# A packing moved to ScalarE and two groups of products moved in TensorE's order, in an attention and FFN kernel

## The chip, the cores and the metric

The kernel runs on one core of one Trainium2 chip. The metric is device time in microseconds (us), lower is better. Before the change the median of the first three runs was 401.98 us (401.9 to 402.39).

The engines have short names in the profile: PE is TensorE (matrix products), PEld its weight loads, DVE is VectorE, ACT is ScalarE, POOL is GpSimd, SP is SyncE. DMA engines move data between HBM and the core; in this kernel SP and POOL issue all of those transfers but the last. "Banks" are the tiles in PSUM into which TensorE writes its products.

## The reference, cut to what matters

```python
k_proj = einsum('ks,bhsd->bhkd', E, k)              # 8 batches, 8 heads, 1024 rows of 64
v_proj = einsum('ks,bhsd->bhkd', F, v)
attn = softmax(q @ k_proj.T / 8)                    # 1024 x 64 a head
x = (attn @ v_proj) as (8192, 512)
out = max(x @ w1, x @ w2, x @ w3) @ w_out           # 512 -> 768 -> 512
```

## The kernel before

The FFN (feed-forward network, the last line above) is most of the work: for each half batch ("chunk", 512 rows) there are six "up" steps of 12 products (2.6 us each) and four "down" steps of 6 (1.3 us each). The attention of the next batch is hung into these steps. TensorE runs its instructions in the order in which the code emits them, so a product that has to wait holds up all that follow: below, the up products behind v of batch 3 do not read v, and yet they start at 129.80, after its wait of 0.71 us.

In the first batch, chunk 1 of q is packed (two heads side by side), transposed on TensorE and copied out. All of this stands between the products with the third up weight:

```python
def pack_q(b, gs, lo, nsi):
    def f():
        ...
        for g in gs:
            copy("v", q_pk[b][:, g, lo:lo + nsi]..., qkv[b][0][:, 2 * g:2 * g + 2, lo:lo + nsi], (), 0.25)
    return f

def qp(b, gs, lo, nsi):             # 8 transposes into a pair of PSUM banks, then one copy to qT on VectorE
    ...
    (2, "a", 0): [pack_q(0, (0, 1), *c1)],     # after the first two products of up step 0 ... 5
    (2, "a", 1): [pack_q(0, (2, 3), *c1)],
    (2, "a", 4): [qp(0, (0, 1), *c1)],
    (2, "a", 5): [qp(0, (2, 3), *c1)],
    (2, 1): [sc(0, 0, *c1)],                   # scores of head pair 0, after up step 1, and so on
    (2, 3): [sc(0, 1, *c1)],
    (2, 4): [za(0, 0, *c1, then=True), sc(0, 2, *c1)],
```

Later batches hang on loads that GpSimd issues, on output stores and on transposes by DMA that SyncE issues:

```python
# plan for batch 1, hung into batch 0 (chunk, step)
(0, 7): [qd(1, 2), za(0, 2, *c1)],   # qd: pack q on VectorE, transpose it by DMA into qT
(0, 8): [za(0, 3, *c1)],
(1, 0): [kproj(1)],                  # needs k of batch 1 in SBUF
(1, 2): [vproj(1), ld(2)],           # needs v of batch 1; ld(2) then loads batch 2 into the same tiles
(1, (3, "mid")): [sc(1, 0, now=True), sc(1, 1)],   # needs qT of batch 1
# plan for batch 3, hung into batch 2
(0, 1): [kproj(3), vproj(3), ld(4)],
(0, 2): [kt(3)],
(0, 3): [sc(3, 0, now=True), sc(3, 1)],
# in down(): after every second down step, 0.5 MB go out
elif tt % 2:
    nc.sync.dma_start(out=ov[:, si - 1:si + 1, :], in_=o_sb)
```

The softmax here doesn't subtract the row's maximum and nothing guards it: scores larger than these inputs give would overflow.

Of the kernel before, what the change touches and what calls it, by code (L numbers as in the profile page):

```python
# [15 lines left out]
def kernel(  # L16
# [70 lines left out]
    def pe(dt, wait=0.0):  # L87
        clock["pe"] = max(clock["pe"], wait) + dt
        return clock["pe"]
# [41 lines left out]
    qkv, qTs, kpTs, vps, pTs, zis, xTs = {}, {}, {}, {}, {}, {}, {}  # L131
# [73 lines left out]
    def scores(b, g, lo, nsi):  # L205
        t, ns = two()
        n = nsi // 2
        for c in range(2):
            for hp in range(2):
                rows = slice(hp * HALF, (hp + 1) * HALF)  # L210
                at = g * SI + lo + c * n
                nc.tensor.matmul(  # L212
                    out=t[c * HALF:(c + 1) * HALF, hp, 0:n * P],
                    lhsT=kpTs[b][rows, g, :],
                    rhs=qTs[b][rows, at:at + n, :],
                    start=True, stop=True,
                )
        return t[:, :, 0:n * P], ns, pe(n * MM / 4 + 0.1)
# [103 lines left out]
    def sc(b, g, lo=0, nsi=SI, now=False):  # L322
        def f():
            t = scores(b, g, lo, nsi)
            if now:
                exps(b, g, lo, nsi, t)
            else:
                later.append(lambda: exps(b, g, lo, nsi, t))
        return f
# [34 lines left out]
    q_pk = {}  # L364

    def pack_q(b, gs, lo, nsi):


        def f():
            if b not in q_pk:  # L370
                q_pk[b] = att.tile([P, NPAIR, SI, 2, D], BF16, name="q_p", bufs=1)
            for g in gs:
                copy(
                    "v", q_pk[b][:, g, lo:lo + nsi].rearrange("p si h d -> p h si d"),
                    qkv[b][0][:, 2 * g:2 * g + 2, lo:lo + nsi], (), 0.25,
                )
        return f

    def qp(b, gs, lo, nsi):
        def f():  # L380
            t, ns = two()
            t = t.bitcast(BF16)[:, 0]
            n = nsi * P
            for i, g in enumerate(gs):
                for si in range(nsi):
                    nc.tensor.transpose(
                        out=t[:, i * n + si * P:i * n + (si + 1) * P],
                        in_=q_pk[b][:, g, lo + si].rearrange("p h d -> p (h d)"),
                        identity=ident,
                    )  # L390
                pe(0.06 * nsi)
            o = qTs[b].rearrange("a (g si) p -> a g si p", si=SI)
            copy(
                "v", o[:, gs[0]:gs[-1] + 1, lo:lo + nsi, :],
                t[:, 0:len(gs) * n].rearrange("a (g si p) -> a g si p", si=nsi, p=P),
                ns, 0.1 + len(gs) * nsi * 0.08,
            )
        return f
# [20 lines left out]
    def kproj(b):  # L419
        def f():  # L420
            t, ns = bank()
            proj(b, 1, t, (LO, HI), 4 * D)
            kps[b] = att.tile([P, 2, 2 * D], BF16, name="kp")
            copy("v", kps[b].rearrange("a g x -> a (g x)"), t[:, 0:4 * D], ns, 0.43)
        return f

    def kt(b):
        def f():
            t, ns = two()
            t = t.bitcast(BF16)[:, 0]  # L430
            for gg in range(2):
                nc.tensor.transpose(
                    out=t[:, gg * P:(gg + 1) * P], in_=kps[b][:, gg, :], identity=ident
                )
            pe(0.2)

            kpTs[b] = att.tile([P, NPAIR, KP], BF16, name="kpT")
            copy(
                "v", kpTs[b].rearrange("a (y x) k -> a x y k", x=2),
                t[:, 0:2 * P].rearrange("a (x y k) -> a x y k", x=2, y=2), ns, 0.3,  # L440
            )
        return f

    def vproj(b):
        def f():
            t, ns = bank()
            proj(b, 2, t, (LO, HI), 4 * D)

            vps[b] = att.tile([P, H, D], BF16, name="vp")
            for hh, hs in enumerate((LO, HI)):  # L450
                i = t[hh * HALF:(hh + 1) * HALF, 0:4 * D].rearrange("a (h d) -> a h d", d=D)
                for to in range(2):
                    copy("sv"[hh], vps[b][to * HALF:(to + 1) * HALF, hs, :], i, ns, 0.4)
        return f
# [250 lines left out]
    def ld(b, which=(0, 1, 2)):  # L705
        return lambda: load(b, which)

    def plan(b):
        n = b + 1
        if b == 0:  # L710
            c1 = (SPC, SPC)
            return {
                (0, 6): [za(0, 1, *c1), sc(0, 3, *c1)],
                (0, 7): [qd(1, 2), za(0, 2, *c1)],
                (0, 8): [za(0, 3, *c1)],
                (1, 0): [kproj(1)],
                (1, 1): [kt(1)],
                (1, 2): [vproj(1), ld(2)],
                (1, (3, "mid")): [sc(1, 0, now=True), sc(1, 1)],
                (1, 4): [za(1, 0), sc(1, 2, now=True)],  # L720
                (1, 5): [za(1, 1), sc(1, 3)],
                (1, 7): [za(1, 2)],
                (1, 8): [za(1, 3)],
            }
        if b == 1:
            return {
                (0, 0): [qd(2)],
                (0, 3): [kproj(2), vproj(2), ld(3, (0,))],
                (0, 4): [kt(2)],
                (0, 5): [sc(2, 0, now=True), sc(2, 1, now=True), sc(2, 2)],  # L730
                (0, 6): [sc(2, 3)],
                (0, 8): [zc(2, nc.gpsimd), ld(3, (1, 2))],
                (1, 1): [qd(3)],
                (1, 3): [vx(2, 0), vx(2, 1)],
                (1, 6): [vx(2, 2), vx(2, 3)],
            }
        if b == 2:
            return {
                (0, 1): [kproj(3), vproj(3), ld(4)],
                (0, 2): [kt(3)],  # L740
                (0, 3): [sc(3, 0, now=True), sc(3, 1)],
                (0, 5): [sc(3, 2, now=True), sc(3, 3)],
                (0, 7): [zc(3)],
                (0, 8): [qd(4)],
                (1, 3): [kproj(4), vproj(4), ld(5), vx(3, 0), vx(3, 1)],
                (1, 4): [kt(4)],
                (1, 7): [vx(3, 2), vx(3, 3), sc(4, 0)],
            }
        if n == B:
            return {}  # L750
        out = {
            (0, 1): [sc(n, 1, now=True), sc(n, 2, now=True), sc(n, 3)],
            (0, 3): [zc(n)],
            (1, 2): [vx(n, 0), vx(n, 1)],
            (1, 6): [vx(n, 2), vx(n, 3)],
        }
        if n + 1 < B:
            out[0, 4] = [qd(n + 1)]
            out[1, 2] = [kproj(n + 1), vproj(n + 1)] + out[1, 2]
            out[1, 3] = [kt(n + 1)]  # L760
            out[1, 6] += [sc(n + 1, 0)]
        if n + 2 < B:
            out[1, 3] += [ld(n + 2)]
        return out

    for b in range(B):
        p = plan(b)

        def behind(ch, step):
            for f in p.get((ch, step), []):  # L770
                f()

        for ch in range(NCHUNK):
            if (b, ch) == (0, 0):
                c1 = (SPC, SPC)
                up_first({
                    (0, 0, 1): [lambda: x(1)],
                    (0, 0, 3): [lambda: z(2), lambda: z(3)],
                    (0, 1, 3): [lambda: v_pair(2), lambda: x(2)],
                    (0, 1, 5): [lambda: v_pair(3), ld(1)],  # L780
                    (0, 2, 1): [lambda: x(3)],
                    (2, "a", 0): [pack_q(0, (0, 1), *c1)],
                    (2, "a", 1): [pack_q(0, (2, 3), *c1)],
                    (2, "a", 4): [qp(0, (0, 1), *c1)],
                    (2, "a", 5): [qp(0, (2, 3), *c1)],
                    (2, 1): [sc(0, 0, *c1)],
                    (2, 3): [sc(0, 1, *c1)],
                    (2, 4): [za(0, 0, *c1, then=True), sc(0, 2, *c1)],
                })
                run_later()  # L790
                behind(0, NJT - 1)
            else:
                for step in range(NJT):
                    up(b, ch, step, lambda: behind(ch, (step, "mid")))
                    behind(ch, step)
            for tt in range(SPC):
                down(b, ch, tt, "v" if b == 0 else "s")
                behind(ch, NJT + tt)
# [30 lines left out]
```

## Time and profile before

| what | before |
|---|---|
| time, first three runs | 401.98 us median |
| time of the profiled execution | 402.96 us (span 401.0) |
| TensorE busy | 392.7 us, 98% |
| DMA engines, first 8 of 40 slices | 90% busy or more |

What TensorE's products waited for, before (total us, times, longest):

```profile
PE banks L346 <- DMA v_t<-in_v_dram: 0.7, 1, 0.7
...
PE banks L212 <- ACT zl L292: 0.5, 1, 0.5
PE banks L490 <- DMA k_t<-in_k_dram: 0.5, 1, 0.5
PE banks L386 <- DVE qT L102: 0.3, 1, 0.3
```

The timeline of TensorE, before, from 34 to 59 us (start, length, engine, line, operation, count; in brackets the idle time before it and what ended that):

```profile
34.66 0.61 PE L386 MATMUL banks<-ident,q_p 128*128 128x128 bf16 x8 [0.35 <-DVE qT L102]
...
39.08 0.30 PE L212 MATMUL banks<-qT,kpT 64*64 64x256 bf16 x4 [0.52 <-ACT zl L292]
...
39.76 1.46 PE L687 MATMUL banks<-wout_sb,hT 128*128 128x512 bf16 x6
...
49.33 1.06 PE L346 MATMUL banks<-k_t,efT 128*64 128x256 bf16 x16
...
55.72 1.06 PE L346 MATMUL banks<-v_t,efT 128*64 128x256 bf16 x16
...
58.55 0.63 PE L212 MATMUL banks<-qT,kpT 64*64 64x512 bf16 x8
```

The second transposes wait for the qT copy, the third scores wait for the Ln (the logarithm of the softmax sums, zl in the profile), the down products start at 39.76. Then k, v and the first scores of batch 1 come at 49.33, 55.72 and 58.55 with no wait. The k and v products of batch 3, in the same view:

```profile
127.03 1.06 PE L346 MATMUL banks<-k_t,efT 128*64 128x256 bf16 x16
128.80 1.06 PE L346 MATMUL banks<-v_t,efT 128*64 128x256 bf16 x16 [0.71 <-DMA v_t<-in_v_dram]
```

The two groups start 1.77 us apart, with a wait for the v load between them. VectorE does the four packings here, as its timeline shows:

```profile
32.82 0.89 DVE L102 COPY q_p<-q_t 128x512 bf16<-128x512 bf16 x4
```

### The profile page before, as it was taken

How to read it: one execution, taken by the hardware profiler on the slowest of the kernel's cores; microseconds unless marked ns; L12 is line 12 of the kernel's file. 1: busy time of each engine (PE TensorE's matmuls, PEld its weight loads, DVE VectorE, ACT ScalarE, POOL GpSimd, SP SyncE). 2: the span in 40 equal slices, each digit the busy share in tenths (PEclk: the TensorE clock that was granted, in tenths of full speed). 3: DMA queues.
4: the chain of work that ended last, by engine and by line, in shares of the span. 5: the costliest groups of instructions: out<-in, count | busy, mean ns of one | idle time of the engine just before them, and what ended most of it. 6: DMA issues, size and time to landing. Idle time of an engine off the chain costs nothing.

```text
span 401.0 us, 5752 instructions
## 1 busy us (share of the span) xinstructions
PE 392.7 (98%) x2286; PEld 176.6 (44%) x2286; DVE 204.1 (51%) x323; ACT 149.0 (37%) x238; POOL 34.4 (9%) x49
## 2 busy tenths in 40 slices
PE   8999999999999999999999999999999999999996
PEld 3444443353444435444454445444454444444443
DVE  2348756761673525746274544744267342745251
ACT  2532438527222452253323542245323533132322
POOL 7440002000400200010020000100000000000000
PEclk9999999999999999999999999999999999999999
DMA  9999999988899998999999959990980229020202
GB/s 154 206 206 207 231 201 145 227 157 158 209 176 209 215 227 181 206 190 210 222 224 172 245 130 268 184 244 24 203 217 1 106 66 253 0 105 2 105 0 105
DMA packets 66330, 66.09 MB, mean 165 GB/s; under 512 B 30624, under 2 KB 58784, under 8 KB 66304
## 3 DMA queue, kind: packets, MB, share of 16 engines
q0 software_dynamic: 29104, 30.41, 47.1%
q1 hardware_dynamic: 37056, 35.20, 34.8%
q8 instruction: 17, 0.28, 0.3%
q10 hardware_dynamic: 144, 0.13, 0.1%
q14 instruction: 9, 0.07, 0.1%
HBM read 69.73 MB, written 16.97 MB: 216 GB/s over the span
## 4 chain that ended last, share of the span: by engine, by line
PE 84%; DMA 8%; DVE 3%; ACT 2%; issue 2%; POOL 1%; DVEq 0%; POOLq 0%; ACTq 0%
PE banks L583 55%; PE banks L687 18%; DMA v_t<-in_v_dram 6%; PE banks L346 3%; PE banks L232 2%; PE banks L212 2%; DMA k_t<-in_k_dram 2%; DVE xT L309 1%; PE banks L257 1%; ACT zl L292 1%; DVE hT L593 1%; ACT zi_all L298 1%; PE banks L490 1%; DVE m L652 0%; PE banks L461 0%
## 5 line engine op out<-in xcount | busy, mean ns | idle before, releaser
L583 PE MATMUL banks<-xT,w_sb 128*128 128x512 bf16 x1152 | 257.6, 379 | 0.3 <-DVE xT L309 0.3
L583 PEld LDWEIGHTS <-w_sb 128*128 128x128 bf16 x1152 | 110.0, 98 | 136.1 <-issue 8.5
L652 DVE TENSOR_TENSOR m<-banks,h1s 128x512 f32<-128x512 f32 x90 | 62.1, 690 | 135.1 <-ACT h1s L648 93.2
L648 ACT COPY h1s<-banks 128x512 f32<-128x512 f32 x90 | 52.7, 586 | 119.2 <-PE banks L583 117.7
L687 PE MATMUL banks<-wout_sb,hT 128*128 128x512 bf16 x378 | 86.9, 380 | 0.1
L593 DVE TENSOR_TENSOR hT<-banks,m 128x512 bf16<-128x512 f32 x90 | 62.3, 692 | 10.1 <-DVE m L652 0.9
L687 PEld LDWEIGHTS <-hT 128*128 128x128 bf16 x378 | 35.2, 98 | 47.7 <-issue 5.8
L102 ACT COPY o_sb<-banks 128x512 f32<-128x512 f32 (+1 forms) x56 | 32.7, 583 | 57.8 <-PE banks L687 57.5
L223 ACT ACTIVATE pT<-banks 128x1024 bf16<-128x1024 f32 (+1 forms) x36 | 32.8, 931 | 26.5 <-PE banks L212 26.5
L309 DVE TENSOR_TENSOR xT<-banks,zi_all 128x1024 bf16<-128x1024 f32 x28 | 33.2, 1220 | 11.7 <-PE banks L232 6.9
L201 POOL DMA_DIRECT2D q_t<-in_q_dram x7 | 6.2, 880 | 194.8 <-DMA qT<-q_p 119.8
L102 DVE CAST vp<-banks 64x256 bf16<-64x256 f32 (+1 forms) x18 | 7.1, 397 | 12.4 <-ACT vp L102 9.3
L346 PEld LDWEIGHTS <-efT 128*64 128x64 bf16 x224 | 11.5, 110 | 4.4 <-issue 3.4
L102 ACT CAST vp<-banks 64x256 bf16<-64x256 f32 x14 | 5.1, 365 | 21.2 <-PE banks L346 21.1
L232 PE MATMUL banks<-pT,vp 64*64 64x512 bf16 (+1 forms) x144 | 11.5, 364 | 0.7 <-DVE vp L102 0.7
L212 PE MATMUL banks<-qT,kpT 64*64 64x512 bf16 (+1 forms) x144 | 11.2, 362 | 0.8 <-ACT zl L292 0.5
L102 DVE COPY q_p<-q_t 128x1024 bf16<-128x1024 bf16 (+1 forms) x32 | 11.3, 417 | 0.0
L292 ACT ACTIVATE zl<-banks 128x512 f32<-128x512 f32 (+1 forms) x12 | 8.9, 740 | 6.4 <-PE banks L232 5.9
L102 DVE COPY o_sb<-banks 128x512 f32<-128x512 f32 (+1 forms) x9 | 5.8, 653 | 4.5 <-PE banks L667 4.5
L461 PE MATMUL banks<-warm_f 128*128 128x512 f32 x8 | 6.6, 977 | 1.5 <-DVE warm_f L175 1.5
L346 PE MATMUL banks<-v_t,efT 128*64 128x256 bf16 x112 | 7.3, 273 | 0.7 <-DMA v_t<-in_v_dram 0.7
L346 PE MATMUL banks<-k_t,efT 128*64 128x256 bf16 x112 | 7.5, 276 | 0.0
(62 smaller groups left out, 119.3 us busy)
## 6 DMA issues: line engine op xcount, KB each, us to landing
out_dram<-o_sb SPq DMA_DIRECT2D x30, 512.0 KB, 4.4
zi_all<-zd SPq DMA_DIRECT2D x20, 512.0 KB, 7.9
q_t<-in_q_dram POOLq DMA_DIRECT2D x7, 1024.0 KB, 9.7
k_t<-in_k_dram POOLq DMA_DIRECT2D x7, 1024.0 KB, 17.2
v_t<-in_v_dram POOLq DMA_DIRECT2D x7, 1024.0 KB, 21.7
zi_all<-zd POOLq DMA_DIRECT2D x4, 512.0 KB, 8.3
w_sb<-in_moe_w_dram POOLq DMA_DIRECT2D x4, 384.0 KB, 11.3
k_t<-in_k_dram POOLq DMA_DIRECT2D x2, 512.0 KB, 8.7
```

The lines of the kernel that those rows point to most:

```text
L102: done = {"v": nc.vector.tensor_copy, "s": nc.scalar.copy, "g": nc.gpsimd.tensor_copy}[eng](out=o, in_=i)
L212: nc.tensor.matmul(out=t[c * HALF:(c + 1) * HALF, hp, 0:n * P], lhsT=kpTs[b][rows, g, :], rhs=qTs[b][rows, at:at + n, :], start=True, stop ...
L223: nc.scalar.activation(out=pTs[b, g, lo], in_=t, func=AF.Exp, scale=scale)
L232: nc.tensor.matmul(out=t[hp * HALF:(hp + 1) * HALF, c, 0:nsi * HALF], lhsT=w(rows, hp), rhs=p[rows, hp, :], start=True, stop=True,)
L292: nc.scalar.activation(out=zl, in_=t, func=AF.Ln)
L309: nc.vector.tensor_tensor(out=xTs[b][:, g, lo:lo + nsi, :].rearrange("a (c s) p -> a c (s p)", c=2), in0=t, in1=zi, op=ALU.mult,)
L346: nc.tensor.matmul(out=t[hh * HALF:(hh + 1) * HALF, 0:width], lhsT=efT[:, si, (kv - 1) * KP:kv * KP], rhs=qkv[b][kv][:, heads[hh], si, :], ...
L583: nc.tensor.matmul(out=h, lhsT=w_sb[i][:, ct, jt * P:(jt + 1) * P], rhs=xTs[b][:, ct, ch * SPC:(ch + 1) * SPC, :], start=(ct == first), st ...
L593: nc.vector.tensor_tensor(out=o, in0=h, in1=other, op=ALU.max)
L648: nc.scalar.copy(out=h1s, in_=h[0][0])
L652: nc.vector.tensor_tensor(out=m12, in0=h[1][0], in1=h1s, op=ALU.max)
L687: nc.tensor.matmul(out=o_ps, lhsT=hTs[b, ch][:, jt, tt * P:(tt + 1) * P], rhs=wout_sb[:, jt, :], start=(jt == 0), stop=(jt == NJT - 1),)
```

## The change

It means to take all three waits away: the packing goes to ScalarE, which was idle then, so that transposes and scores can come earlier and further from what frees their banks; the products of batch 3 come one up step later, when their data has landed.

```diff
             for g in gs:
                 copy(
-                    "v", q_pk[b][:, g, lo:lo + nsi].rearrange("p si h d -> p h si d"),
-                    qkv[b][0][:, 2 * g:2 * g + 2, lo:lo + nsi], (), 0.25,
+                    "s", q_pk[b][:, g, lo:lo + nsi].rearrange("p si h d -> p h si d"),
+                    qkv[b][0][:, 2 * g:2 * g + 2, lo:lo + nsi], (), 0.58,
                 )
@@ plan of batch 3
-                (0, 1): [kproj(3), vproj(3), ld(4)],
-                (0, 2): [kt(3)],
-                (0, 3): [sc(3, 0, now=True), sc(3, 1)],
+                (0, 2): [kproj(3), vproj(3), ld(4)],
+                (0, 3): [kt(3)],
+                (0, 4): [sc(3, 0, now=True), sc(3, 1)],
@@ first chunk
-                    (2, "a", 4): [qp(0, (0, 1), *c1)],
+                    (2, "a", 3): [qp(0, (0, 1), *c1)],
-                    (2, 3): [sc(0, 1, *c1)],
+                    (2, 2): [sc(0, 1, *c1)],
```

The last argument of the copy (0.25, 0.58) only feeds a clock in the code that chooses PSUM banks while it records the program.

## The prediction

> **What bounds the kernel.** TensorE: the page gives PE 98% busy (392.7 of 401.0 us), VectorE 51%, ScalarE 37%, full granted clock; 84% of the chain of waits is PE. A 128x512 product starts every 0.216 us. The change adds and removes no product, so it can win only time in which PE stands still near what it touches. Steps between product starts (timeline), less the usual step, show:
> - 33.93: the second packed q transposes wait 0.5 us for VectorE's qT copy (33.91 to 34.60) to free their banks.
> - 38.27: scores wait 0.7 us for ScalarE's Ln (38.44 to 39.03) to free theirs.
> - 127.82: v of batch 3 stands 0.87 us longer than in other batches (waits list: 0.7), for a load that lands at 128.76.
>
> **Moved.** Four packings of 128x512 bf16 leave VectorE (32.82 to 33.71) for ScalarE, which idles there for 9.8 us. The Trainium skill, "ScalarE: Activation LUTs", section "What ACT_TABLE_LOAD costs", gives 186 ns + 0.833 ns an element, 93 ns less back to back: estimated 0.61 us, pitch 0.52. This trace agrees: a ScalarE cast of that size from SBUF took 0.619 us. q's second chunk lands at 31.68, so packings end near 32.3, 32.8, 33.3, 33.85. The first transposes, two products earlier (32.84), find their data; the second come at 34.2 instead of 34.66: PE leads by 0.43 us. The second scores, moved up, wait for the first exponential in their banks (to 36.6), which gives back 0.2. The third take banks freed by VectorE's max operations, by the built order, at 38.2: no wait. Estimated lead when the down products start (39.76 before): 0.85 us.
>
> **Given back.** v of batch 1 lands at 55.19 by a DMA queue that PE does not drive, and PE uses it at 55.72, so 0.85 of lead makes a new wait of 0.3 to 0.5. I keep 0.4.
>
> **Batch 3.** k and v products come one FFN step (2.6 us) later, near 130, after the landing: the 0.87 us vanish. Scores go from step 3 to 4; the four exponentials (1.03 us each, between copies of 0.59) still end in time for the sum products at 144.3. The load of batch 4 is hardly later, since its q part waits for transposes landing at 130.71 anyway. Narrow: the transposed q of batch 4 lands at 169.12 and its scores run at 169.37. It hangs on SyncE's queue (reciprocal out 146.58, back 151.56, transposes 154.43 to 167.15), which should move up with PE, but in DMA traffic that does not. I take 0.2 us back.
>
> **Sum.** 0.4 + 0.87 - 0.2 = about 1.1 us of 402: predicted 400.9 us, range 400.1 to 401.9. Faster by over 2%: 0.5%; within 2%: 99%; slower by over 2%: 0.5%.
>
> **What would show it.** Timeline: ScalarE copies q_p<-q_t from 31.7 to 33.9; no 0.5 us hole at the second transposes, no 0.7 us hole before the third scores; down products from about 38.9. PE's waits: no v_t wait near 128, perhaps one of up to 0.5 near 55, perhaps one for qT near 168. VectorE busy 0.9 us less, ScalarE 2.2 more.
>
> **What would make it wrong.** The v load of batch 1 landing later, because output and transposes start earlier, or not binding (then 400.4). The bank choice, which shifts for the whole kernel, making a new wait in batch 3's scores. The transposed q of batch 4 not moving up at all (401.4).

## More of the kernel before

The profile is one execution, and here the profiled one was slower than all three timed runs.

The page of the kernel before: first line the span; then busy time of each engine; then the span in 40 slices (9 means 90% or more) for the granted TensorE clock and the DMA engines.

```profile
span 401.0 us, 5752 instructions
...
PE 392.7 (98%) x2286; PEld 176.6 (44%) x2286; DVE 204.1 (51%) x323; ACT 149.0 (37%) x238; POOL 34.4 (9%) x49
...
PEclk9999999999999999999999999999999999999999
DMA  9999999988899998999999959990980229020202
```

TensorE is nearly always busy and its clock is full, so only its idle moments can be won. The DMA row is the second thing to see: through the first eight slices (80 us) the DMA engines are full as well.

## The result

The changed kernel took 402.94 us (median of 4 runs, 402.87 to 403.61) against 402.19 us (4 runs, 401.9 to 402.69) of the kernel before. A ratio here is the mean time of one kernel's runs over that of the other's of the same rounds, so it is not quite the ratio of the medians: 1.0021, 95% interval 1.0004 to 1.0038. The change made the kernel a little slower.

The profile after, page and TensorE's waits:

```profile
span 400.4 us, 5708 instructions
...
PE 388.4 (97%) x2244; PEld 176.7 (44%) x2286; DVE 203.5 (51%) x319; ACT 151.0 (38%) x242; POOL 34.2 (9%) x49
```

```profile
PE banks L346 <- DMA v_t<-in_v_dram: 1.0, 1, 1.0
PE banks L490 <- DMA k_t<-in_k_dram: 0.9, 1, 0.9
...
PE banks L212 <- ACT pT L223: 0.2, 1, 0.2
```

The span of this profile is 0.6 us shorter than that of the profile before, while the timed runs are 0.75 us longer. The two single profiles mislead. TensorE's busy time is no help either: it fell by 4.3 us although no product was removed, but 42 of 2286 product records are missing from this trace (all 2286 weight loads are there), so the two cannot be compared. The Trainium skill, "Trainium Kernel Development and Optimization", section "Performance Expectations", calls matmul busy time a bad metric for how close a kernel is to its limit, for another reason (products are pipelined); no run here tests that reason.

ScalarE's and TensorE's timelines, after:

```profile
31.56 2.18 ACT L102 COPY q_p<-q_t 128x512 bf16<-128x512 bf16 x4 [5.00 <-DMA q_t<-in_q_dram]
```

```profile
32.78 0.61 PE L386 MATMUL banks<-ident,q_p 128*128 128x128 bf16 x8
...
34.17 0.61 PE L386 MATMUL banks<-ident,q_p 128*128 128x128 bf16 x8
...
36.58 0.30 PE L212 MATMUL banks<-qT,kpT 64*64 64x256 bf16 x4 [0.16 <-ACT pT L223]
...
38.02 0.48 PE L212 MATMUL banks<-qT,kpT 64*64 64x256 bf16 x4
...
38.88 1.46 PE L687 MATMUL banks<-wout_sb,hT 128*128 128x512 bf16 x6
...
48.44 1.06 PE L346 MATMUL banks<-k_t,efT 128*64 128x256 bf16 x16
...
55.95 1.06 PE L346 MATMUL banks<-v_t,efT 128*64 128x256 bf16 x16 [1.04 <-DMA v_t<-in_v_dram]
...
58.77 0.63 PE L212 MATMUL banks<-qT,kpT 64*64 64x512 bf16 x8
```

The first half works as meant. The four packings run from 31.56 to 33.74, the hole before the second transposes is gone, the third scores no longer wait for the Ln, the down products start at 38.88. But then v of batch 1 brings a new wait of 1.04 us, and the scores of batch 1 start at 58.77, later than the 58.55 of before. Batch 3, after:

```profile
129.84 1.06 PE L346 MATMUL banks<-k_t,efT 128*64 128x256 bf16 x16
130.74 1.04 PE L346 MATMUL banks<-v_t,efT 128*64 128x256 bf16 x16
```

k and v groups are 0.90 us apart: no wait.

### The profile page after: what moved, and what is told of

Its sections match the earlier page's. It is cut to its first block, busy times and chain, and to the rows that moved or that the text cites. A ratio compares the mean times of both kernels' runs of the same rounds, so it can differ in the third digit from the quotient of the medians.

```text
span 400.4 us, 5708 instructions
## 1 busy us (share of the span) xinstructions
PE 388.4 (97%) x2244; PEld 176.7 (44%) x2286; DVE 203.5 (51%) x319; ACT 151.0 (38%) x242; POOL 34.2 (9%) x49
## 3 DMA queue, kind: packets, MB, share of 16 engines
q1 hardware_dynamic: 37056, 35.20, 34.3%
## 4 chain that ended last, share of the span: by engine, by line
PE 84%; DMA 9%; DVE 2%; issue 2%; ACT 1%; POOL 0%; DVEq 0%; ACTq 0%; POOLq 0%
PE banks L583 56%; PE banks L687 18%; DMA v_t<-in_v_dram 8%; PE banks L346 3%; PE banks L232 2%; PE banks L212 2%; DMA k_t<-in_k_dram 2%; DVE xT L309 1%; PE banks L257 1%; ACT zi_all L298 1%; ACT zl L292 1%; PE banks L490 1%; DVE m L652 0%; PE banks L461 0%; PE banks L516 0%
## 5 line engine op out<-in xcount | busy, mean ns | idle before, releaser
L583 PE MATMUL banks<-xT,w_sb 128*128 128x512 bf16 x1119 | 254.8, 379 | 2.6 <-issue 0.8
L687 PE MATMUL banks<-wout_sb,hT 128*128 128x512 bf16 x370 | 85.6, 379 | 1.0 <-issue 0.8
L102 DVE COPY q_p<-q_t 128x1024 bf16<-128x1024 bf16 x28 | 10.4, 435 | 0.5 <-DMA q_t<-in_q_dram 0.5
```

The source lines that it names most:

```text
L102: done = {"v": nc.vector.tensor_copy, "s": nc.scalar.copy, "g": nc.gpsimd.tensor_copy}[eng](out=o, in_=i)
L583: nc.tensor.matmul(out=h, lhsT=w_sb[i][:, ct, jt * P:(jt + 1) * P], rhs=xTs[b][:, ct, ch * SPC:(ch + 1) * SPC, :], start=(ct == first), st ...
L687: nc.tensor.matmul(out=o_ps, lhsT=hTs[b, ch][:, jt, tt * P:(tt + 1) * P], rhs=wout_sb[:, jt, :], start=(jt == 0), stop=(jt == NJT - 1),)
```

## The experiments

**A common clock.** The first loads land at different moments in each execution, so the first k product of batch 0 starts anywhere from 9.64 to 10.54 us in the 14 profiles. All columns of the next table but the last count from that product (times read from the traces, landings included). The last column is the distance from the first k to the first v product of batch 3; undisturbed it is 0.90.

| profile | order in the first chunk | k 1 lands | v 1 lands | down starts | v 1 products | scores 1 | batch 3, k to v |
|---|---|---|---|---|---|---|---|
| before (first profile) | old | 37.87 | 45.55 | 30.12 | 46.08 | 48.90 | **1.77** |
| e1_null | old | 37.67 | 45.90 | 29.99 | 45.95 | 48.78 | 0.90 |
| e1_batch3 | old | 37.95 | 45.64 | 30.21 | 46.17 | 49.00 | 0.90 |
| e2_pack_only | old | 37.84 | 46.07 | 29.99 | 46.11 | 48.94 | 0.90 |
| e3_before_defer | old | 37.31 | 43.38 | 29.99 | 45.95 | 48.78 | 0.90 |
| e1_start | new | 37.43 | 45.98 | 29.16 | 46.02 | 48.85 | 0.90 |
| after (first profile) | new | 38.06 | 46.20 | 29.18 | 46.25 | 49.08 | 0.90 |
| e1_both | new | 38.70 | 46.66 | 29.32 | 46.70 | 49.53 | 0.90 |
| e3_both | new | 38.73 | 46.63 | 29.39 | 46.67 | 49.50 | 0.90 |
| e2_start_hold | new | 39.53 | 45.20 | 29.17 | 45.96 | 48.79 | 0.90 |
| e3_both_hold | new | 37.35 | 45.04 | 29.16 | 45.12 | 47.95 | 0.90 |
| e3_both_defer | new | 37.67 | 44.12 | 29.16 | 45.12 | 47.95 | 0.90 |

The two profiles with v products moved are told of where they were run. After the scores of batch 1, all profiles in this table need 338.0 to 338.3 us to the last product, but for the first one, which needs 338.92. From the start of the last product to the end of the span it is 3.5 to 3.6 us in all of them but e2_pack_only (5.0). So this table, with the start of the first k product, holds nearly all that tells the kernels apart. Every row is one execution, and not always a typical one: those of e1_both, e2_pack_only and e2_both_vlate were the slowest of their runs.

### e1_null: the kernel before against itself

No edit.

> The kernel before, unchanged, timed against itself: what two equal kernels show. Both theories: ratio 1.000 within 0.1%. Theory T (transfers): the landing of v for batch 3 differs from execution to execution; if this profile shows a shorter v wait near 128 than the 0.7 us of the first profile, that profile was a slow one (it took 402.96 where the timed runs took 401.9 to 402.69) and the second half of the change has less to win in a usual run. Theory O (overhead outside the span): time minus span is about 2.0 us here and about 2.4 in the changed kernel, in every run.

Measured: ratio 1.0002 (0.9990 to 1.0014). Batch 3 in this profile's TensorE timeline:

```profile
127.18 1.06 PE L346 MATMUL banks<-k_t,efT 128*64 128x256 bf16 x16
128.07 1.04 PE L346 MATMUL banks<-v_t,efT 128*64 128x256 bf16 x16
```

The same program, and the wait for v is not there. Of the seven profiles of kernels that leave batch 3 where it was, only the very first shows it: v of batch 3 landed 119.12 us after the first k product there and at 117.86 here. Theory O is not borne out as it was put: time minus span was 1.74 to 2.42 us in these runs and 1.74 to 2.57 in those of the changed kernel beside them, not 2.4 in every one. A small part is not excluded: the means of time minus span were 2.08 and 2.07 us in e1_both and e3_both, and 1.87 and 1.83 in the runs of before beside them.

### e1_both, e3_both: the changed kernel again

No edit to the changed kernel.

> The changed kernel again. On record: ratio 1.0021. Theory T: between 0.999 and 1.002, by where v of batch 1 lands; the profile again shows a v wait near 55 and none near 128, and time minus span is that of the null run. Theory O: ratio 1.002 again with a span that is shorter than the null run's.

> The changed kernel once more, beside the three. Theory D: ratio 1.001 to 1.002, v wait near 55 of 1.0 to 1.4 us, no wait near 128.

Measured: 1.0015 (1.0003 to 1.0027) and, on another chip, 1.0012 (0.9997 to 1.0027), with v waits of 1.4 and 1.3 us and none in batch 3. With the first result, the small loss shows in three sets of runs, each with runs of before of its own; in the last the interval just includes 1. TensorE's waits in e1_both:

```profile
PE banks L346 <- DMA v_t<-in_v_dram: 1.4, 1, 1.4
```

### e1_start and e1_batch3: one half each

The first has only the packing and first-chunk edits; the second only the edits to the plan of batch 3.

> The first half alone: packing on ScalarE and the transposes and scores moved up; batch 3 as before. Theory T: the lead of 0.85 us at 39 is lost whole at the v wait near 55, and more when the transfers that start earlier delay v; ratio 1.000 to 1.002, v wait near 55 of 0.8 to 1.1 us, v wait near 128 still there if the null run has it. Rival R (the lead survives): ratio 0.998.

> The second half alone: k, v products and scores of batch 3 one step later. Theory T: the v wait near 128 is gone, no other wait comes; ratio 0.998 if the usual run of before waits 0.9 us there, 1.000 if it does not. Rival: the moved products themselves cost, by the banks dealt anew for all that follows; ratio over 1.001 with new waits after 128.

Measured: the first half alone 1.0020 (1.0005 to 1.0035), v wait 0.8 us; the second half alone 1.0000 (0.9988 to 1.0012), no new wait. From the waits of the first half alone:

```profile
PE banks L346 <- DMA v_t<-in_v_dram: 0.8, 1, 0.8
```

The loss comes from the first half, and the second half wins nothing in a usual run because the wait that it removes is usually not there.

### e2_pack_only: the packing alone

```diff
-                    "v", q_pk[b]...
+                    "s", q_pk[b]...
```

> The packing alone on ScalarE, no transposes or scores moved. All theories: the packings end at 33.7 to 33.9, as late as on VectorE, so PE's step over the second transposes is as long or 0.1 us shorter, and the wait for the Ln (0.7 us) stays; down products start at 39.7 as before; ratio 1.000. If they start by 39.2, the engine and not the order made the lead.

Measured: 1.0002 (0.9984 to 1.0021), down products at 29.99 by the common clock, as in the old order. The engine alone makes no lead; it takes the new places of transposes and scores, and the packing on ScalarE is not late for them. The new places with the packing left on VectorE were not run, so whether the move to ScalarE was needed is not shown.

### e2_both_vlate and e2_before_vlate: v of batch 1 one step later

```diff
-                (1, 2): [vproj(1), ld(2)],
+                (1, 3): [vproj(1), ld(2)],
```

> The changed kernel, with v products of batch 1 (and the load of batch 2 that follows them) one FFN step, 2.6 us, later. Theory T (the lead of the first half is lost whole at the v load of batch 1, which lands at 55.2 to 56.4 whatever PE does): no v wait near 55; k products and all that follows keep the lead of 0.85 us; ratio 0.998, span 0.7 to 0.9 us under that of before. Rival L (the lead would be lost at the next transfer anyway, transposed q of batch 1 or 4, or was no lead): ratio 1.000 or over, with another wait in v's place.

> The kernel before with that same move alone. Theory T: PE comes to v at 55.7 to 55.9 and waits little there (0 to 0.2 us), so ratio 0.9995 to 1.000. If this is as fast as the run with the change, the gain is the move's own and not the lead's.

Measured: 1.0004 (0.9980 to 1.0027) with the change and 1.0005 (0.9988 to 1.0022) without. The expected 0.998 lies at the edge of the first interval, so the times alone do not exclude the theory that the one v wait holds the whole lead. What speaks against it is the profile, though of the slowest of the six executions (404.86 us). Its timeline of TensorE:

```profile
49.95 1.06 PE L346 MATMUL banks<-k_t,efT 128*64 128x256 bf16 x16 [1.06 <-DMA k_t<-in_k_dram]
...
58.68 0.63 PE L212 MATMUL banks<-qT,kpT 64*64 64x512 bf16 x8 [0.54 <-DMA qT<-q_p]
```

k and the transposed q of batch 1 wait in v's place. The wait for the transposed q is not owed to the lead alone: the kernel before with this edit lists it as well, with 0.5 us. In these profiles the load to blame is not one load: everything that batch 1 needs arrives just in time.

### e2_start_hold and e3_both_hold: the transposes of batch 1 a step later

```diff
-                (0, 7): [qd(1, 2), za(0, 2, *c1)],
-                (0, 8): [za(0, 3, *c1)],
+                (0, 7): [za(0, 2, *c1)],
+                (0, 8): [za(0, 3, *c1), qd(1, 2)],
```

> The first half of the change, with packing and DMA transposes of batch 1's q one down step later (about 1.3 us), nothing else. Theory E (earlier transposes of q take DMA time from the load of v for batch 1, so v lands 0.3 to 0.6 us later than in the kernel before): v lands again at 55.2 to 55.8, ratio falls from 1.002 to 1.000. Rival N (v lands when it lands, differences of 0.5 us between profiles are noise): v landing 55.9 to 56.4 as in the first half alone, ratio 1.001 to 1.002.

> The changed kernel with packing and transposes of batch 1's q one down step later. Theory D: v back at 55.3, but k a little late, as in the first half alone with the same edit (ratio 0.9985 there): ratio 0.998 to 1.000, span 0.3 us or more under the changed kernel's in this call.

Measured: 0.9985 (0.9969 to 1.0001) for the first half with this edit and 0.9978 (0.9964 to 0.9992) for the whole change with it. With this edit the first of the two transposes is issued at 37.5 by the common clock, and not at 34.2 to 34.5. In both profiles v lands at 45.0 to 45.2 instead of 46.0 to 46.7. So the landing that theory E expected came, and not the one of rival N. In the first, k was late (39.53, a wait of 0.8 us), and the scores of batch 1 came no sooner (48.79) than in the old order; that execution had the longest span of its six (400.5, the others 399.8 to 400.3). In the second nothing was late. The kernel before with this edit alone was not run. TensorE's timeline of the second:

```profile
49.06 1.06 PE L346 MATMUL banks<-k_t,efT 128*64 128x256 bf16 x16
...
55.45 1.06 PE L346 MATMUL banks<-v_t,efT 128*64 128x256 bf16 x16
...
58.28 0.63 PE L212 MATMUL banks<-qT,kpT 64*64 64x512 bf16 x8
```

### e3_both_defer and e3_before_defer: the first store later

The first 0.5 MB of output wait for the issue of the second; nothing else moves.

```diff
         elif tt % 2:
-            nc.sync.dma_start(out=ov[:, si - 1:si + 1, :], in_=o_sb)
+            held.append((ov[:, si - 1:si + 1, :], o_sb))
+            if (b, ch, tt) != (0, 0, 1):
+                for o, i in held:
+                    nc.sync.dma_start(out=o, in_=i)
+                held.clear()
```

> The changed kernel, with the first output store (0.5 MB, issued at 43 to 44 us on the queue that shares the DMA engines with the loads of batch 1) held back to the issue of the second one, after the transposes. Theory D (from 44 to 56 the DMA engines are full, so the lead of 0.85 us at the down products turns into waits at k, v or transposed q of batch 1): k and v of batch 1 land 1 to 2.6 us earlier (v by 54.5), no wait over 0.2 us at any of the three, lead kept at 60; span 0.7 to 0.9 us under before, ratio 0.998. Rival L (the lead is lost later, at batch 2 or 3): ratio 1.000 with v early.

> The kernel before with the held store alone. Theory D: v also lands by 54.5, but PE does not come before 55.7, so nothing is won: ratio 0.9995 to 1.000. If it is 0.998, the store was worth it by itself.

Measured: 0.9982 (0.9966 to 0.9999) with the change, 0.9994 (0.9979 to 1.0008) without. v lands at 44.12 and 43.38. With the change, k, v and scores of batch 1 run with no wait:

```profile
48.79 1.06 PE L346 MATMUL banks<-k_t,efT 128*64 128x256 bf16 x16
...
55.18 1.06 PE L346 MATMUL banks<-v_t,efT 128*64 128x256 bf16 x16
...
58.01 0.63 PE L212 MATMUL banks<-qT,kpT 64*64 64x512 bf16 x8
```

Without the change v also lands early, but TensorE comes no sooner (v products at 45.95), and little or nothing is won. So the lead is real: with the store held back, the scores of batch 1 start 0.83 us sooner with the change than without (47.95 and 48.78). The timed means of the two, 402.00 and 402.58 us, differ by 0.58 us, which six runs each do not set clear of noise. What is clear of it is the cost of the late transfers: on one chip, in one set of runs, the changed kernel took 403.32 us on average, with the transposes later 401.95 and with the store later 402.00 (six runs each; I estimate the 95% intervals of the two differences at 0.7 and 0.8 us either way). Those 1.3 to 1.4 us are about the size of its v wait.

Where the DMA time went shows in the queues in the same stretch, 44 to 52 us (q0 are the loads that GpSimd issues, q1 stores and transposes that SyncE issues; packets, MB, time of their packets as a share of that of the 16 engines; the times of packets overlap, so the shares can add up to more than 100%). First the changed kernel, then the same with the transposes a step later, then with the store held back:

```profile
q0 software_dynamic: 1205, 1.22, 90.3%
q1 hardware_dynamic: 617, 0.65, 28.9%
```

```profile
q0 software_dynamic: 1353, 1.37, 102.3%
q1 hardware_dynamic: 176, 0.53, 18.2%
```

```profile
q0 software_dynamic: 1441, 1.45, 107.9%
q1 hardware_dynamic: 629, 0.16, 14.5%
```

What q1 does not take in this stretch, the loads get: 1.22, 1.37 and 1.45 MB. In the kernel before it was this:

```profile
q0 software_dynamic: 1251, 1.26, 94.1%
q1 hardware_dynamic: 483, 0.61, 25.7%
```

These stretches count from the start of each span. By the common clock, from 34.3 to 42.3 us, the loads of the same four got 1.22, 1.33, 1.39 and 1.27 MB: the same order, with smaller steps.

The traces also tell store and transposes apart, by the size of their packets (4096 and 256 bytes). From 36 to 41 us by the common clock, in the profiles that leave the store where it was:

| transposes of batch 1 | packets of the store | packets of the transposes | loads, MB |
|---|---|---|---|
| a step later (2 profiles) | 128 | 0 | 0.76 |
| old order (5) | 128 | 116 to 150 | 0.70 to 0.72 |
| new order (5) | 128 | 246 to 279 | 0.67 to 0.68 |

Each five includes one of the two with v products moved. The store takes the same in all three, so what the new order takes from the loads in this stretch, it takes by its earlier transposes.

## Why the prediction was wrong

- **What bounds the kernel: right.** TensorE does, and only its idle moments could be won.
- **Cost of the packing on ScalarE: right.** One took 0.614 us at a pitch of 0.52, as estimated from the Trainium skill, "ScalarE: Activation LUTs", section "What ACT_TABLE_LOAD costs". The last ended at 33.74, 0.1 us before the predicted 33.85.
- **Lead of 0.85 us at the down products: right.** By the common clock they start at 29.16 to 29.39 in the new order and at 29.99 to 30.21 in the old. The small wait of the second scores for the first exponential came too.
- **"So 0.85 of lead makes a new wait of 0.3 to 0.5. I keep 0.4": wrong; this is one of the two steps that failed.** The place was right, the size was not. From the start of the down products to the scores of batch 1 an undisturbed kernel takes 18.79 us; the four profiles of the new order that have no other edit took 19.69 to 20.21. So 0.9 to 1.4 us were lost, more than the whole lead. The prediction held v's landing fixed, at that of one profile, and named earlier output and transposes only as a risk. By the common clock v lands at 45.55 to 46.07 in four of the old order that leave store and v products alone (mean 45.79), and at 45.98 to 46.66 in these four (mean 46.37, from 45.98, 46.20, 46.66 and 46.63). The one profile at hand had the earliest of the old landings. An undisturbed new order comes to v at 45.12, so an estimate from the old mean is a wait of 0.7 us already; the later landing adds 0.6. The two groups touch (46.07 and 45.98), so the shift rests on eight profiles and on the edits that move it. The store and the first transposes start 0.85 us sooner with TensorE, at a time when k and v still load (the packet counts above show what the loads then lose to the transposes). The Trainium skill, "DMA: Bandwidth & Descriptors", section "Issuing engines are not separate DMA queues", says that transfers of all issuers interleave on the same 16 engines; the runs with the store or the transposes later agree, with v at 44.12 and 45.04.
- **"The 0.87 us vanish": wrong for a usual run; the other step.** The wait of batch 3 was in one of seven profiles. It was read from the one profile at hand, of an execution of 402.96 us where the timed runs took 401.9 to 402.39: a sign that was there to be read. The second half alone measured 1.0000.
- **0.2 us back at the transposed q of batch 4: came in one execution of four.** The lists leave out waits under 0.15 us, but the steps from one product's start to the next show it: undisturbed, the scores of batch 4 start 0.205 us after the product before them; in the new order it was 0.205 in e1_start, 0.206 in e3_both, 0.237 in the first profile (q landed at 168.67, used at 168.71) and 0.474 in e1_both. It is not the change's own: e3_before_defer, in the old order, shows 0.404.
- **The sum.** Predicted: 0.4 + 0.87 - 0.2 = 1.1 us faster. Shown: 0.85 - (0.9 to 1.4) + 0 - (0 to 0.3) = about 0.05 to 0.8 us slower. The timed ratios of 1.0012 to 1.0021 are 0.5 to 0.8 us, in the upper part of this; whether a small part lies outside the span (2.07 to 2.08 against 1.83 to 1.87 us, above) was not separated from noise, since executions of the unchanged kernel beside them had spans of 400.0 to 402.8 us.

Why v of batch 3 was late in one execution stays open. So does how the late v divides between store and transposes: the counts from 36 to 41 us point to the transposes, but moving either one let v land early. That k landed at 39.53 in one held run and at 37.35 in the other is also not explained.

The version with the change and the transposes of batch 1 one down step later is the fastest measured, 0.9978 of the kernel before (0.9964 to 0.9992). Whether its gain owes anything to the batch 3 half was not told apart: without that half the ratio was 0.9985, within the interval.

## What to carry to other kernels

A stall that is removed is worth only what the next stalls let through; where TensorE and the DMA engines are both near full, look up when the data of the next stage lands and how much later it is used before counting a lead, and ask which transfers the faster engine will itself start sooner. A wait seen in one profile of one execution is not yet a cost: compare that execution's time with the timed runs and profile the same kernel twice. When a small gain is lost at a full set of DMA engines, moving an unhurried store or transpose behind the hurried loads can release it.

## What the Trainium skill lacked or had wrong

- "TensorE: Matmul & The Clock Gate", section "Back-to-back issue gap", gives about 131 ns a product for a sustained stream of weight load and product at N=512. Here the median step from one 128x512 bf16 product to the next was 216 ns, each with its weight load, at full clock; the formula given there for an isolated product, N/2.4 + 2.5 ns, fits (215.8).
- "DMA: Bandwidth & Descriptors", section "Issuing engines are not separate DMA queues", says that transfers interleave but not what that costs a load in flight. Here a 0.5 MB store moved out of the way let the load of v land about 2.2 us sooner in the new order (46.37, the mean of four profiles, to 44.12 in one, by the common clock) and 2.4 us sooner in the old (45.79 to 43.38).
- No page that I read tells of the spread between executions of one program on one core: spans of 400.1 to 402.8 us in twelve runs of the kernel before, and a load of batch 3 that landed 1.3 us apart in two profiles of it.
